# Delta-rule attention feeding a squared-ReLU MLP on one core: when the MLP's weights are split, by which engine, and in whose scratch

## The chip, the cores and the metric

One NeuronCore of a Trainium2 chip runs the whole program. The metric is device time in microseconds (us). The engines are TensorE (PE in the profile, its weight loads PEld), VectorE (DVE), ScalarE (ACT), GpSimd (POOL) and the queue of SyncE (SP), which issues nearly all DMAs.

## The reference

There are 4 batches of 8 heads, 768 time steps and head dimension 48, all float32.

```python
k_n = k / (norm(k) + 1e-6)
for t in range(768):                       # for each batch and head; state is 48 x 48
    y[t] = q[t] @ state
    v_old = state.T @ k_n[t]
    state += beta[t] * outer(k_n[t], v[t] - v_old)
x = y as (3072 tokens, 384)                # 8 heads x 48
out = square(max(x @ w_in, 0)) @ w_out     # w_in 384 x 2048, w_out 2048 x 384
```

## The kernel before, in words

**Attention.** Time is cut into 12 units of 64 steps, and two units make a pair. For a pair, `key_products` (L377) multiplies the keys with themselves on PE and copies four sets of blocks out of PSUM (`copies`, by ACT, DVE or both, after the string `A["copies"]`). `prepare` (L417) turns one result on DVE and makes norms and betas. `invert` (L468) inverts 32-row triangles by substitution, two DVE instructions a step. `ended` (L496) scales and turns the inverse. For the first pair alone (FAST), `invert` works on 16-row halves in 15 steps (31 for the other pairs), and `corrected` (L520) joins the halves: PE, a copy on ACT, PE twice more, then two DVE subtractions into `tt` and `t1` (L542, L543). `below` (L547; `below_both` for later pairs) makes the blocks under the diagonal. `query_products` (L600), `scale_v` (L625) and `state_part` (L635) then give a unit's `w`, the new state and `y`, strictly in order of units.

**MLP.** `moe(u)` (L688) takes the 256 tokens of unit u. Every float32 operand is the sum of a high and a low fp32r part, and each product is three matmuls. For each of 8 blocks `fp` it forms h (L735), evacuates it by three ACT passes (L742, L743, L745) and one DVE pass (L710, `rest`), and two blocks later multiplies by w_out (L719, `second`).

**Weights.** The weights come in 17 parts (`weight_parts`), 14 of 768 columns and 3 of 512, in the order in which moe(0) wants them. `fetch` issues their DMAs on SP. `split_weights` is a generator that turns a raw part into its high and low half:

```python
ACT  a    = |raw| * 2**-112              # L222   (magnitude)
ACT  tail = low bits of raw, scaled      # L224   (magnitude)
DVE  a = (a << 3) | tail                 # L252   join 1
DVE  a = (raw & sign) | a                # L257   join 2
ACT  high = a as fp32r                   # L260
low = a - high: DVE, L238 (mode "d"), or PE twice and an ACT copy, L234 and L236 (mode "t", parts 0 to 3)
```

`a` lies in a ring of three buffers and `tail` in one of two, so a part's two ACT passes run at most two parts ahead of its joins. `half_of` makes moe wait, at build time, until a part's steps have been issued.

**Order.** PE, SP, DVE and ACT run in the order in which the program is written (`manual_schedule`). The first unit is issued by the string `A["order"]`, a letter per piece (A and B key products, P prepare, I a step of the inverse, e ended, c corrected, b below, V scale_v, s state_part); after piece n, `A["fill"][n]` steps of the split are issued, 40 of its 51 before moe(0) begins. From unit 1 on, `weave` sorts pieces of attention and of the MLP of the unit before by the fractions in `A`: moe(0) is woven with attention of unit 1, moe(1) with unit 2, and so on. The rest of the splits and the first pair's `corrected` and `below` of unit 1 lie in the first weave, and the second pair's inverse (31 steps) in the first and second; in the second weave, `below_both` waits for `ended` of that pair.

## Time and profile before

| | |
|---|---|
| median of 3 runs | 607.59 us (607.03, 607.59, 609.38) |
| profiled execution | 606.13 us, of which the span from first to last instruction is 604.4 us |
| PE busy, mean granted clock | 557.8 us (92%), 0.964 of full speed |
| DVE busy, ACT busy, POOL busy | 393.3 us (65%), 331.0 us (55%), 49.2 us (8%) |
| DMA | 37.77 MB, mean 62 GB/s |

A row of the timeline gives start and duration in us, engine, line, operation and operands; square brackets hold the engine's idle time just before the row and what ended it. Line numbers are those of the kernel before. A row of the windows gives, for a stretch, its length and for each engine the busy time and the number of instructions in brackets, then the granted TensorE clock, the DMA share and GB/s.

### The profile page before, as it was taken

What the parts mean: (1) busy time and instruction counts of PE and PEld (TensorE: products, weight loads), DVE (VectorE), ACT (ScalarE), POOL (GpSimd) and SP (SyncE); (2) the same over time, 40 slices, a digit from 0 to 9 for tenths busy, and PEclk for the clock granted to TensorE, in tenths of its full rate; (3) what the DMA queues carried; (4) which work ended last, traced back from release to release, by engine and by line L of the source; (5) the groups of instructions that cost most, each with busy time, mean ns of one, the idle gap of its engine ahead of it and who ended that gap; (6) DMA issues with size and microseconds to landing.
All of it is one profiled execution on the core that took longest, in us unless ns stands there. A gap on an engine that the chain in (4) does not pass through costs nothing.

```text
span 604.4 us, 23205 instructions
## 1 busy us (share of the span) xinstructions
PE 557.8 (92%) x10520; PEld 535.2 (89%) x10520; DVE 393.3 (65%) x709; ACT 331.0 (55%) x521; POOL 49.2 (8%) x62
## 2 busy tenths in 40 slices
PE   4554589999999999999999999999999999999997
PEld 3434479999999999999999999999999999999997
DVE  2996986989446989257988348996548895421111
ACT  4774987444646454557354556355456365454442
POOL 3110000200101102002002002002002002001000
PEclk9695599999999999999999999999999999999999
DMA  8996160032243050253050251140450320200101
GB/s 245 301 264 218 23 114 3 2 69 41 29 74 62 2 102 6 29 88 49 9 99 2 43 92 30 35 73 3 65 81 19 61 48 4 49 8 2 27 1 26
DMA packets 146674, 37.77 MB, mean 62 GB/s; under 512 B 140272, under 2 KB 143344, under 8 KB 146576
## 3 DMA queue, kind: packets, MB, share of 16 engines
q1 hardware_dynamic: 146496, 36.20, 29.4%
q8 instruction: 82, 1.34, 0.9%
q14 instruction: 16, 0.13, 0.1%
q10 hardware_dynamic: 80, 0.10, 0.0%
HBM read 31.56 MB, written 4.72 MB: 60 GB/s over the span
## 4 chain that ended last, share of the span: by engine, by line
PE 88%; ACT 3%; DVE 3%; DMA 2%; SPq 2%; issue 2%; DVEq 0%; ACTq 0%
PE h L735 35%; PE o L719 32%; PE g L719 2%; PE g L655 2%; PE g L645 2%; PE g L607 2%; PE g L680 2%; PE g L661 2%; PE g L387 2%; PE g L673 2%; SPq L304 1%; PE h L695 1%; DMA tt<-in_k_dram 1%; DMA ap<-in_k_dram 1%; PE g L538 1%
## 5 line engine op out<-in xcount | busy, mean ns | idle before, releaser
L719 PE MATMUL o<-w,h_h 128*128 128x384 f32 x704 | 185.5, 344 | 0.0
L735 PE MATMUL h<-x_h,w 128*128 128x256 f32 x1152 | 170.5, 283 | 2.3 <-DVE x_l L698 1.7
L735 PEld LDWEIGHTS h<-x_h,w 128*128 128x128 f32 x1152 | 154.4, 190 | 4.0 <-ACT x_h L697 2.6
L710 DVE TENSOR_TENSOR h_l<-r,h_h 128x512 fp32r<-128x512 f32 x96 | 68.3, 715 | 116.4 <-ACT h_h L745 116.4
L742 ACT ACTIVATE r<-h 128x512 f32<-128x512 f32 x96 | 57.4, 598 | 124.4 <-PE h L735 111.6
L719 PEld LDWEIGHTS o<-w,h_h 128*128 128x128 f32 x704 | 121.2, 189 | 2.2
L719 PE MATMUL o<-w,h_l 128*128 128x384 f32 x352 | 118.2, 336 | 0.0
L735 PE MATMUL h<-x_l,w 128*128 128x256 f32 x576 | 100.4, 283 | 0.6 <-issue 0.6
L735 PEld LDWEIGHTS h<-x_l,w 128*128 128x128 f32 x576 | 82.6, 191 | 0.8 <-issue 0.8
L719 PEld LDWEIGHTS o<-w,h_l 128*128 128x128 f32 x352 | 66.1, 188 | 0.0
L743 ACT ACTIVATE r<-r 128x512 f32<-128x512 f32 x96 | 60.7, 633 | 3.1
L745 ACT CAST h_h<-r 128x512 fp32r<-128x512 f32 x96 | 59.6, 621 | 3.0
L491 DVE TENSOR_TENSOR z<-z,tmp 128x31 f32<-128x31 f32 (+15 forms) x155 | 53.2, 343 | 5.3
L489 DVE TENSOR_TENSOR tmp<-lt,z 128x31 f32<-128x31 f32 (+15 forms) x155 | 52.6, 340 | 3.8
L613 POOL TENSOR_SCALAR_AFFINE_SELECT ap<-ap 64x1024 f32<-64x1024 f32 x24 | 30.6, 1277 | 242.7 <-ACT ap L610 241.9
L676 DVE TENSOR_TENSOR state<-state,g 48x768 f32<-48x768 f32 x22 | 20.9, 950 | 21.0 <-PE g L673 20.9
L683 ACT COPY y<-g 128x768 f32<-128x768 f32 x12 | 9.6, 800 | 38.7 <-PE g L680 38.7
L434 POOL MEMSET z<- 128x1024 f32 x5 | 4.8, 953 | 233.9 <-DVE lt L422 191.9
L697 ACT CAST x_h<-h 128x384 fp32r<-128x384 f32 x24 | 11.4, 481 | 19.2 <-PE h L695 19.2
L698 DVE TENSOR_TENSOR x_l<-h,x_h 128x384 fp32r<-128x384 f32 x24 | 13.0, 556 | 13.3 <-ACT x_h L697 12.9
L260 ACT CAST w<-a 128x768 fp32r<-128x768 f32 (+1 forms) x17 | 13.4, 796 | 9.7 <-DVE a L257 9.7
L661 PE MATMUL g<-vt,tt 64*64 64x48 f32 x768 | 14.8, 225 | 3.1 <-ACT tt L566 3.1
(152 smaller groups left out, 707.8 us busy)
## 6 DMA issues: line engine op xcount, KB each, us to landing
w<-in_moe_w_out_dram SPq DMA_DIRECT2D x8, 768.0 KB, 9.5
w<-in_moe_w_in_dram SPq DMA_DIRECT2D x6, 768.0 KB, 7.2
vt<-in_v_dram SPq DMA_DIRECT2D x48, 96.0 KB, 3.0
kp<-in_k_dram SPq DMA_DIRECT2D x48, 96.0 KB, 3.1
out_dram<-rest SPq DMA_DIRECT2D x47, 96.0 KB, 2.2
kb<-in_q_dram SPq DMA_DIRECT2D x40, 64.0 KB, 2.4
kb<-in_k_dram SPq DMA_DIRECT2D x32, 64.0 KB, 2.7
w<-in_moe_w_in_dram SPq DMA_DIRECT2D x3, 512.0 KB, 5.1
```

The source lines that it names most:

```text
L260: nc.scalar.copy(out=hl[:, 0], in_=a.bitcast(F32))
L489: nc.vector.tensor_tensor(out=tmp, op=ALU.mult, in0=lt[:, s:s + 1, s + 1:].broadcast_to([P, nj, nt]), in1=z[:, :nj, s:s + 1].broadcast_to( ...
L491: nc.vector.tensor_tensor(out=z[:, :nj, s + 1:], in0=z[:, :nj, s + 1:], in1=tmp, op=ALU.subtract)
L613: nc.gpsimd.affine_select(out=half, in_=half, pattern=[[0, 2 * X], [1, C]], base=0, channel_multiplier=-1, compare_op=ALU.is_gt, fill=0.0)
L661: nc.tensor.matmul(ps[half_rows(b ^ j), j, x], lhsT=t[half_rows(b), j, x], rhs=vt[half_rows(b), j, x], start=True, stop=True)
L676: nc.vector.tensor_tensor(out=s[dims(j)], in0=s[dims(j)], in1=ps[dims(j)], op=ALU.add)
L710: nc.vector.tensor_tensor(out=h_l, in0=r, in1=h_h.bitcast(F32), op=ALU.subtract)
L719: nc.tensor.matmul(o[i], lhsT=a[:, e, i * P:(i + 1) * P], rhs=w_[w], start=(ft == 0 and n == 0), stop=(ft == FT - 1 and n == 2))
L735: nc.tensor.matmul(hp[:, e], lhsT=half_of(("wi", kt, part))[w][:, f], rhs=x[:, kt], start=(n == 0), stop=(n == 3 * KT - 1))
L742: nc.scalar.activation(out=r, in_=hp, func=AF.Relu)
L743: nc.scalar.activation(out=r, in_=r, func=AF.Square)
L745: nc.scalar.copy(out=h_h, in_=r)
```

## The change

The split's two ACT passes (`magnitude`) leave the generator of the joins. They get their own counts, `A["fillm"]`, and may run far ahead: parts 0 to 4 put `a` and `tail` not into the rings but into the rooms of parts 8, 9, 10, 11 and 15, which are fetched only after the owner's halves are made. The raw parts 8 to 16 are therefore issued one or a few at a time as parts 0 to 4 end, no longer 17 in one go ahead of `corrected`.

Engines are chosen per part by three letters: the magnitude (A is ACT, D is DVE), the cast to the high half (A or D), the low half (D is DVE, P is PE). Of 17 parts, three magnitudes (parts 1, 4, 8) and six casts (3, 5, 6, 8, 11, 13; the last of 512 columns) go from ACT to DVE, as `tensor_scalar` from SBUF to SBUF. The low halves on PE go from four parts to three (0, 1, 10). In the key products of the first pair one set of copies goes from DVE to ACT, in those of the second pair the set shared by both goes to ACT. One scaling of `goff` and one pair of upper copies in `below` go from ACT to DVE; the zeroing of `tt` goes from ACT to GpSimd.

In `corrected` the t1 product and subtraction are left out for the lower 32 rows of each 64: half of the L539 matmuls go, and one DVE subtraction on 128 partitions becomes two on 32. The first inverse and its scaled copy lie in a room of their own (`small`, zeroed and set by GpSimd at the start; it is the room of part 16). In unit 0 the state update follows y. The order string, all fractions and the fills are new: 26 of the 51 steps come before moe(0), the other 25 in the first 0.04 to 0.27 of the first weave. The string of `order` has 15 steps of the inverse as before.

```diff
-          'copies': {0: 'ADDA', 1: 'DADB', 2: 'ABDA'},
+          'copies': {0: 'DAAA', 1: 'DADA', 2: 'ABDA'},
-          'fill': [0, 0, 2, 2, 0, 1, 1, 1, 0, 0, 0, 0, 0, 0, 0, 0, 0, 0, 0, 0, 0, 0, 1, 1, 0, 1, 0, 0, 0, 0, 0, 0, 0, 2,
-                   0, 0, 1, 0, 0, 0, 1, 1, 1, 3, 3, 3, 0, 2, 2, 8, 3],
+          'fill': [0, 0, 0, 0, 1, 0, 0, 0, 0, 0, 1, 1, 0, 0, 1, 0, 0, 0, 0, 0, 0, 0, 0, 0, 0, 0, 0, 1, 0, 0, 0, 1, 1, 0,
+                   1, 0, 0, 0, 0, 0, 0, 0, 1, 4, 3, 1, 3, 0, 2, 3, 1],
+          'fillm': [0, 0, 1, 0, 0, 1, 0, 1, 0, 0, 0, 0, 0, 1, 0, 0, 0, 1, 0, 0, 0, 0, 1, 0, 1, 0, 0, 0, 0, 1, 1, 2, 0, 0,
+                    0, 2, 0, 0, 2, 0, 0, 1, 0, 0, 1, 1, 2, 0, 0, 2, 2],
-          'mode': 'ttttddddddddddddd',
+          'mode': ['AAP', 'DAP', 'AAD', 'ADD', 'DAD', 'ADD', 'ADD', 'AAD', 'DDD', 'AAD', 'AAP', 'ADD', 'AAD', 'ADD',
+                   'AAD', 'AAD', 'AAD'],
-          'order': '-01lABBTPAAPPBPP2xPPIIIGIIyZIIIPIIIIIIIeeeecccVbbss',
+          'order': '01-AlBPBPBTxAAPPGP2PPPIIIIIZIIIIIIIIyIIeeeecccbVbss',
...
+    room_of = {x: r for x, r in zip(range(NW), wide_rooms) if r >= x + A["rooms"]}
+    owner = {r: x for x, r in room_of.items()}
...
-            if x < NW:
+            if x < NW and (x not in owner or weight_parts[owner[x]][0] in halves) and (x < NW - 1 or ("ended", 0) in done):
...
+        if x in room_of:
+            both = wpool.tile([P, 2, n], I32, name=f"w{room_of[x]}")
+            a, tail = both[:, 0], both[:, 1]
+        else:
             a = spool.tile([P, PC], I32, name="a", bufs=3)[:, :n]
             tail = spool.tile([P, PC], I32, name="rest", bufs=2)[:, :n]
+        if A["mode"][x][0] == "D":
+            nc.vector.tensor_scalar(out=a.bitcast(F32), in0=raw[:, :, 1].bitcast(F32), scalar1=2.0 ** -112,
+                                    scalar2=None, op0=ALU.mult)
+        else:
             nc.scalar.activation(out=a.bitcast(F32), in_=raw[:, :, 1].bitcast(F32), func=AF.Abs, scale=2.0 ** -112)
...
-            nc.scalar.copy(out=hl[:, 0], in_=a.bitcast(F32))
-            if x + 2 < NW:
-                fetch(max(0, min(x + A["ahead"], NW) - len(raws)))
-                ready[x + 2] = magnitude(x + 2)
+            if A["mode"][x][1] == "D":
+                nc.vector.tensor_scalar(out=hl[:, 0], in0=a.bitcast(F32), scalar1=1.0, scalar2=None, op0=ALU.mult)
+            else:
+                nc.scalar.copy(out=hl[:, 0], in_=a.bitcast(F32))
...
-                    nc.tensor.matmul(ps[r, j, 1, x], lhsT=z[r, j, x], rhs=yt[r, j, x], start=True, stop=True)
+                    if n % 2 == 0:
+                        nc.tensor.matmul(ps[r, j, 1, x], lhsT=z[r, j, x], rhs=yt[r, j, x], start=True, stop=True)
...
-        nc.vector.tensor_tensor(out=t1[:, :, i, :, :QB], in0=t1[:, :, i, :, :QB], in1=ps[:, :, 1, :, :QB], op=ALU.subtract)
+        for b in range(2):
+            nc.vector.tensor_tensor(out=t1[up(b), :, i, :, :QB], in0=t1[up(b), :, i, :, :QB], in1=ps[up(b), :, 1, :, :QB],
+                                    op=ALU.subtract)
...
+        if not first:
+            update()
...
         nc.scalar.copy(out=y.rearrange("p n (q j e) -> p j (n q) e", j=2, e=D), in_=gy)
+        if first:
+            update()
...
+            magnitudes(next(fillm, 0))
             take(splits, next(fill, 0))
```

## Rows read from the trace of the kernel before

**Rows 1.** The page's span and its 40 slices of 15.1 us each.

```profile
span 604.4 us, 23205 instructions
...
PE   4554589999999999999999999999999999999997
...
DVE  2996986989446989257988348996548895421111
...
PEclk9695599999999999999999999999999999999999
```

**Rows 2.** Windows, by stage of the opening and after it, all engines.

```profile
27.30:40.80 13.50, 7.76 (x94) 5.78 (x93) 12.49 (x35) 10.86 (x17) 3.40 (x3) 0.94 1.06 333
...
46.20:57.60 11.40, 6.17 (x384) 5.68 (x384) 6.09 (x7) 5.22 (x7) 0.00 (x0) 0.50 0.74 280
57.60:66.20 8.60, 2.46 (x128) 2.06 (x128) 8.53 (x11) 6.79 (x10) 0.00 (x0) 0.50 0.02 4
66.20:78.50 12.30, 7.88 (x326) 7.09 (x327) 10.88 (x15) 10.86 (x17) 0.00 (x0) 0.71 0.39 73
78.50:88.90 10.40, 9.29 (x306) 8.82 (x307) 10.23 (x15) 9.31 (x15) 0.00 (x0) 1.00 0.60 99
88.90:97.70 8.80, 8.80 (x253) 8.32 (x255) 2.01 (x4) 7.02 (x13) 0.00 (x0) 1.00 0.12 15
97.70:153.70 56.00, 56.00 (x903) 54.87 (x894) 52.31 (x104) 27.49 (x45) 6.75 (x6) 1.00 0.18 31
153.70:604.40 450.70, 444.39 (x7975) 431.06 (x7974) 270.29 (x492) 233.15 (x368) 32.51 (x26) 1.00 0.24 41
```

**Rows 3.** Groups by line, 0 to 95 us: busy us, mean ns | idle before.

```profile
L257 DVE SCALAR_TENSOR_TENSOR a<-w,a 128x768 int32<-128x768 int32 (+1 forms) x17 | 15.4, 909 | 0.4
L252 DVE SCALAR_TENSOR_TENSOR a<-a,rest 128x768 int32<-128x768 int32 (+1 forms) x17 | 15.4, 906 | 1.4 <-ACT rest L224 1.3
L222 ACT ACTIVATE a<-w 128x768 f32<-128x768 f32 (+1 forms) x17 | 14.8, 871 | 2.1 <-PE o L234 1.7 <-DVE w L238 0.2
...
L260 ACT CAST w<-a 128x768 fp32r<-128x768 f32 (+1 forms) x17 | 13.4, 796 | 9.7 <-DVE a L257 9.7
L238 DVE TENSOR_TENSOR w<-a,w 128x768 fp32r<-128x768 f32 (+1 forms) x13 | 11.5, 891 | 0.0
```

**Rows 4.** Timeline of DVE at the end of the first correction.

```profile
57.64 0.42 DVE L542 TENSOR_TENSOR tt<-tt,g 128x256 f32<-128x256 f32 x1 [5.28 <-PE g L539]
57.98 0.41 DVE L543 TENSOR_TENSOR t<-t,g 128x256 f32<-128x256 f32 x1
...
60.04 0.95 DVE L252 SCALAR_TENSOR_TENSOR a<-a,rest 128x768 int32<-128x768 int32 x1
60.91 0.96 DVE L628 TENSOR_TENSOR vt<-vt,nr 128x768 f32<-128x768 f32 x1
```

**Rows 5.** Chain of waits, 40 to 92 us: start, us, what.

```profile
50.24 2.98 issue
...
55.20 1.48 issue
```

**Rows 6.** Timeline of DVE from the second pair's key products.

```profile
97.72 0.69 DVE L402 COPY z<-g 128x512 f32<-128x512 f32 x1 [4.46 <-PE g L387]
98.45 1.39 DVE L404 COPY z<-g 32x512 f32<-32x512 f32 x2
...
102.01 1.40 DVE L399 COPY mt<-g 32x512 f32<-32x512 f32 x2
```

**Rows 7.** Timeline, the narrow DVE instruction with a constant.

```profile
25.42 0.18 DVE L443 TENSOR_SCALAR n<-s 128x32 f32<-128x32 f32 x1
```

**Rows 8.** Timeline where the second pair's inverse is handed to PE.

```profile
151.62 2.06 DVE L516 STREAM_TRANSPOSE t<-z 128x1024 f32<-128x1024 f32 x1
...
155.73 0.21 PE L577 MATMUL g<-tt,mt 32*32 32x32 f32 x1
```

**Rows 9.** Timeline, the first MLP matmul of the kernel.

```profile
78.52 0.95 PE L735 MATMUL h<-x_h,w 128*128 128x256 f32 x6 [1.70 <-DVE x_l L698]
```

## The prediction, made before the changed kernel ran

> **What bounds the kernel now.** I read the page's slices first [rows 1]: PE is full from slice 7 to the last, and all that is not full lies in the first six slices, some 91 us. There DVE's digits are the high ones, with a 4 at 45 to 60 us and a 3 at 91 to 106 us. So the end of the run is set by how early PE becomes full, and by what it must still wait for after that.

> Then the windows by stage [rows 2]. After 153.7 us PE is busy for 444.4 of 450.7 us, and part of the rest is the tail. At most a few us are to be had there; I count nothing for the new fractions of the later units. From 97.7 to 153.7 us PE is busy for 56.00 of 56.00 us, while DVE is busy for 52.31: DVE works at its limit on the second pair (preparation, 31 steps of the inverse, its turning), and hands over in time by little. The last turning ends at 151.62 + 2.06 = 153.7 us and PE's first matmul on it starts at 155.73 [rows 8]; PE had other work till then and lost nothing. If PE comes to that place earlier, it waits for DVE. So two clocks run in this opening: PE's, which starts with the first MLP matmul at 78.5 us [rows 9], and DVE's, which must end its work on the second pair. The later of the two decides.

> Of DVE's clock the windows show the holes. Between 27.3 and 153.7 us it is idle for 5.3 us in the first correction (6.09 busy of 11.40), for 6.8 us between the last weight and the second pair's key products (2.01 of 8.80), and in no other stage for more than about 1 to 4 us. Rows of the timeline give the same two: 5.28 us until PE's L539 ends [rows 4], 4.46 us until PE's L387 ends [rows 6].

> **The change, step by step, on DVE.** Into the holes goes weight work: 14 of the 51 steps, some 12 us at 0.87 each (below), that stood ahead of moe(0) now stand behind it. In the correction the fills put ten weight instructions on DVE (one after the turning, then 5, 4 and 1 steps' worth), some 8 us, where before DVE waited 5.3; and 25 steps instead of 11 lie in the first weave, so that DVE is still on weights when PE reaches the key products. I let 1 us of the 12.1 stay: 11.1 us won.

> What it adds to DVE until the second pair is turned:
> - Nine passes come from ACT. The trace has no wide DVE instruction with one SBUF input and a constant. From below they cost 0.18 us, the narrow one with a constant [rows 7]; from above 0.87 us, the distance of two wide ones that follow each other (60.04, 60.91) [rows 4]. The one row is near in kind and the other in width, so I take the middle, 0.52: 4.7 us (1.6 to 7.8).
> - One low half more on DVE (14 instead of 13): 0.87, as the distance above.
> - One goff scaling of 256 columns: 0.4, as L543 [rows 4]; from below 0.2.
> - The t1 subtraction, twice: one instruction of 0.41 becomes two on 32 partitions with as many columns. L404 takes 1.39 for two on 32 partitions, L402 0.69 for one on 128 of the same width [rows 6]: fewer partitions save nothing. 0.8.
> - Two upper copies of 512 columns: 0.69 each from PSUM as L404 [rows 6], by the narrow row 0.18 each: I take 0.9 for both (0.4 to 1.4).
> - Copies that leave: one set of the first pair, 0.69 + 1.39 = 2.1, and DVE's half of a set of the second, 1.4 (L399) [rows 6].

> Sum: 4.7 + 0.87 + 0.4 + 0.8 + 0.9 - 2.1 - 1.4 = 4.2 us more (0.4 to 7.8). DVE ends the second pair 11.1 - 4.2 = 6.9 us earlier (3.3 to 10.7). Against it stands that PE has more of its work behind that place: the fractions put it at (0.4682 - 0.0044) / 0.5731 = 81% of moe(1)'s pieces before and at (0.5355 - 0.0272) / 0.648 = 78% after; 2.5% of 31 pieces. From 78.5 us to the end twelve units take 525.9 us, 43.8 each, with 34 pieces and the attention in them, so a piece is at most 1.3 us and this at most 1.0, which I take. Net on this clock: 5.9 us (2.3 to 9.7).

> [...]

> **On PE's clock.** Ahead of the first correction (46.2 us) the letters and fills put 6 joins in place of 11, two moved passes, one copy set less and one scaling more: 5 x 0.87 + 2.1 - 1.0 - 0.4 = 5.0 us less DVE work; the first part of it waits for loads and ACT in any case, so I take 3.6. The correction lasts 11.4 us, of which PE stands 2.98 + 1.48 us at "issue" [rows 5] with nothing to wait for; 64 of its 384 instructions go, of 6.17 us busy [rows 2]: 1.0 us. From there to the state (8.60 us) DVE has 1.2 of corrections, 4.0 of weights and 0.9 for the values, 6.1: 2.5 us less. From the state to the first MLP matmul (12.30 us, DVE busy 10.88) DVE has 9.2: 1.7 us less. That is 8.8 us: the MLP starts at 69.7. From there the first three MLP blocks and the second correction need little of DVE, but each evacuation and h_l stands behind some weight steps. I take 0.5 us off: PE is 8.3 us ahead when it comes to the second pair. There it finds DVE only 5.9 ahead.

> **What costs nothing, and why.** The copies that ACT gains: it loses nine passes at about 0.8 to 0.9 [rows 3] and was busy for 5.22 of 11.40 in the correction [rows 2]; if that cover went, relu of moe(0) would come late by as much. The late fetches: a room is free when its owner's low half is made, parts 8 to 10 are issued from the inverse to the correction and the rest in it, and their ACT passes come at 60 us and later. The DMA engines stand at 0.02 in 57.6 to 66.2 us [rows 2], so there is room; if a part came late, ACT would wait with w and y queued behind that pass, and PE for them. On SP, values and keys of unit 0 now stand ahead of those parts instead of behind, which can only help. GpSimd's zeroing and setting run where it was idle. The state update moved behind y leaves 1.5 to 2 us of PE and DVE work to the time after y, where nobody waits before unit 1's state.

> **The sum.** The profiled execution: 606.13 - 5.9 = 600.2 (span 604.4 - 5.9 = 598.5 and 1.73 around it). The lowest of the runs shown lies 0.9 above the profiled execution (607.03), the median 1.5; I add 0.9: **601.1 us**.

> **Rivals.**
> 1. *PE's clock decides.* If the moved passes cost less than about 0.26 us, DVE adds under 9 x 0.26 - 0.5 = 1.8 us, and PE no longer waits at the second pair. For it: 0.18 for the narrow one [rows 7]. Against: 768 columns are 24 times as many. 606.13 - 8.3 + 0.9 = 598.7.
> 2. *DVE gets back what the holes give.* Passes at 0.87, and half of the correction's hole stays (2.6 us) since the joins there wait for ACT's passes or PE stands longer at "issue": 11.1 - 2.6 - (7.8 - 0.5) - 1.0 = 0.2, 606.8; with the passes alone 604.2, with the hole alone 603.7. For it: ACT stood 9.7 us waiting for L257 and DVE 1.3 us for L224 [rows 3], so the two engines do hold each other up. Against: ACT's passes now run ahead. No real gain, then: the work has only moved.
> [...]

> **Chances.** Forecast 0.45 (its own range 598.5 to 604.2), rival 1 0.19, rival 2 0.24, rival 3 0.12. The runs of this kernel differ by 0.4% and a median can tell some 0.5% (3 us) from no change. Faster by more: 0.44 + 0.19 + 0.04 of rival 2's lower end = 0.67; within: 0.01 + 0.20 = 0.21; slower: rival 3's 0.12. The range leaves out rival 3 and a little at the lower end: 596.5 to 607.2, which takes in both ends of DVE's added work, 606.8 of rival 2 and 2 us below rival 1.

> **What the new profile would show.** Right: DVE without a hole over 2 us from 13 us to the second pair's turning, that turning at about 147 us; the first MLP matmul at about 70; PE full until the place of `below_both` in the second weave and there a wait of some 2 us on DVE; moved passes near 0.5 us. Wrong: passes at 0.9 us or 0.2 us; "issue" waits over 5 us in the correction; ACT waiting for a late weight part; a granted clock of 0.50 after 85 us.

## The result, and the profile after

| | before | after |
|---|---|---|
| median | 608.68 us (606.52 to 610.15, 11 runs) | 601.58 us (599.99 to 605.94, 11 runs) |
| ratio after/before, 95% interval | | 0.9897, 0.9875 to 0.9918 |
| profiled execution, its span | 606.13, 604.4 us | 601.16, 599.4 us |

The kernel became 1.0% faster; 601.1 us was forecast. The page of the kernel after answers to [rows 1]; its slices are 15.0 us each.

```profile
span 599.4 us, 22921 instructions
...
PE   5655899999999999999999999999999999999997
...
DVE  2999599999347988348988448896548895421111
...
PEclk9675699999999999999999999999999999999999
```

DVE's two digits of 6 at 45 to 60 and 91 to 106 us (the prediction called them 4 and 3; the row has 6 in both) are 9 now, and one 5 has come at 60 to 75 us. PE is full from slice 6 on, not 7. The windows say by how much; they answer to [rows 2], with stages of the new kernel (columns as there).

```profile
40.00:60.00 20.00, 11.38 (x536) 10.07 (x536) 19.60 (x26) 9.01 (x13) 0.00 (x0) 0.53 0.77 277
...
68.00:76.00 8.00, 6.93 (x163) 6.44 (x165) 4.25 (x8) 3.02 (x5) 0.00 (x0) 0.57 0.72 134
...
85.00:96.00 11.00, 11.00 (x192) 10.71 (x190) 10.90 (x16) 10.84 (x18) 0.00 (x0) 1.00 0.21 25
96.00:112.00 16.00, 13.83 (x206) 12.86 (x205) 15.45 (x26) 10.84 (x19) 4.95 (x4) 1.00 0.01 2
149.50:599.40 449.90, 444.52 (x7981) 431.34 (x7980) 270.70 (x491) 233.30 (x368) 31.65 (x26) 1.00 0.24 41
...
13.10:149.46 136.36, 112.13 (x2299) 101.83 (x2292) 125.75 (x225) 85.82 (x134) 12.25 (x10) 0.84 0.46 120
```

The last row runs from DVE's first work to the end of the second pair's turning. The same stretch before ended at 153.68 and had DVE busy for 121.56 of 140.58 us: DVE has 4.2 us more work and 8.4 us less idle time. After 149.5 us hardly anything changed: PE is busy for 444.52 of 449.90 us, before 444.39 of 450.70 [rows 2], so this part is 0.8 us shorter. In 85 to 96 us PE, DVE and ACT are all full; in 96 to 112 us PE is idle for 2.2 us, where before it was never idle.

The timeline of DVE shows the moved pass, the two holes of more than 1 us that are left, and the turning; it answers to [rows 4, 8].

```profile
59.44 0.96 DVE L294 SCALAR_TENSOR_TENSOR a<-w,a 128x768 int32<-128x768 int32 x1
60.43 0.56 DVE L298 TENSOR_SCALAR w<-a 128x768 fp32r<-128x768 f32 x1
62.79 1.92 DVE L722 TENSOR_TENSOR state<-state,g 48x768 f32<-48x768 f32 x2 [1.80 <-PE g L719]
...
73.67 0.42 DVE L585 TENSOR_TENSOR tt<-tt,g 128x256 f32<-128x256 f32 x1 [3.65 <-PE g L580]
74.01 0.85 DVE L587 TENSOR_TENSOR t<-t,g 32x256 f32<-32x256 f32 x2
...
147.41 2.05 DVE L558 STREAM_TRANSPOSE t<-z 128x1024 f32<-128x1024 f32 x1
```

PE's timeline at the first MLP matmul, at the transposes of unit 1's y (my landmark for the experiments; 126.2 us before) and where the second pair's inverse reaches it, beside [rows 8, 9]:

```profile
69.44 0.58 PE L786 MATMUL h<-x_h,w 128*128 128x256 f32 x1
...
121.37 0.49 PE L746 MATMUL h<-eye,y 128*128 128x128 f32 x3
...
151.21 0.21 PE L622 MATMUL g<-tt,mt 32*32 32x32 f32 x1
```

PE is 9.1 us ahead at the first (78.52 before), 4.8 at the second, 4.5 at the third (155.73), and 5.0 at the end. So half of the early start is lost again before 121 us. The chain of waits shows where it runs:

```profile
47.44 7.75 DMA w<-in_moe_w_in_dram
...
67.55 1.52 issue
69.51 2.22 PE h L786 x9
73.60 2.15 PE h L786 x9
...
78.77 1.85 PE g L275 x6
80.61 1.08 PE h L786 x9
...
90.51 0.96 DVE a L294
```

From 59 to 83 us the end hangs mostly on PE: with "issue" (idle time for which the profile shows no releaser), with two groups of nine matmuls at a granted clock of 0.50 and 0.55 (2.22 and 2.15 us, against 1.08 for nine at 1.00), and with the low half of weight part 10 (L275). From 85 to 100 us it hangs on DVE alone. Ahead of that the chain passes through the late load of weight part 8 (first line): it landed at 55.19 us and DVE began on it at 55.25. DVE was busy for 19.60 of the 20.00 us around it, so nothing was lost, but this load has no room left.

### The profile page after: what moved, and what is told of

Read it like the earlier page. It is cut to its first block, busy times and chain, and to the rows that moved or that the text cites. A ratio compares the mean times of both kernels' runs of the same rounds, so it can differ in the third digit from the quotient of the medians.

```text
span 599.4 us, 22921 instructions
## 1 busy us (share of the span) xinstructions
PE 563.3 (94%) x10386; PEld 539.1 (90%) x10386; DVE 398.6 (66%) x719; ACT 324.1 (54%) x510; POOL 51.2 (9%) x63
## 3 DMA queue, kind: packets, MB, share of 16 engines
q8 instruction: 81, 1.33, 0.9%
## 4 chain that ended last, share of the span: by engine, by line
PE 81%; DVE 7%; DMA 2%; issue 2%; ACT 1%; SPq 0%
PE h L786 33%; PE o L770 29%; PE g L770 2%; PE g L700 2%; PE g L729 2%; PE g L690 2%; PE g L719 2%; PE g L706 2%; PE g L652 2%; PE g L431 1%; DMA w<-in_moe_w_in_dram 1%; PE h L746 1%; DVE w L279 1%; PE g L811 1%; DVE t L558 1%
## 5 line engine op out<-in xcount | busy, mean ns | idle before, releaser
L786 PE MATMUL h<-x_h,w 128*128 128x256 f32 x1152 | 172.5, 286 | 1.7 <-DVE x_l L749 1.1
L761 DVE TENSOR_TENSOR h_l<-r,h_h 128x512 fp32r<-128x512 f32 x96 | 65.5, 686 | 111.0 <-ACT h_h L796 110.9
L534 DVE TENSOR_TENSOR z<-z,tmp 128x31 f32<-128x31 f32 (+15 forms) x155 | 55.1, 355 | 5.3
L532 DVE TENSOR_TENSOR tmp<-lt,z 128x31 f32<-128x31 f32 (+15 forms) x155 | 54.5, 352 | 3.7
L749 DVE TENSOR_TENSOR x_l<-h,x_h 128x384 fp32r<-128x384 f32 x24 | 13.0, 556 | 12.1 <-ACT x_h L748 11.8
L729 PE MATMUL g<-w,ap 64*64 64x48 f32 x768 | 14.6, 226 | 1.7 <-ACT w L709 1.4
```

Source lines behind the costliest of these rows:

```text
L532: nc.vector.tensor_tensor(out=tmp, op=ALU.mult, in0=lt[:, s:s + 1, s + 1:].broadcast_to([P, nj, nt]), in1=z[:, :nj, s:s + 1].broadcast_to( ...
L534: nc.vector.tensor_tensor(out=z[:, :nj, s + 1:], in0=z[:, :nj, s + 1:], in1=tmp, op=ALU.subtract)
L729: nc.tensor.matmul(gy[half_rows(b), j, x], lhsT=ap[0][half_rows(b ^ j), j, x], rhs=w[half_rows(b ^ j), j, x], start=first and x == 0, stop ...
L761: nc.vector.tensor_tensor(out=h_l, in0=r, in1=h_h.bitcast(F32), op=ALU.subtract)
L786: nc.tensor.matmul(hp[:, e], lhsT=half_of(("wi", kt, part))[w][:, f], rhs=x[:, kt], start=(n == 0), stop=(n == 3 * KT - 1))
```

## The experiments

Each kernel is the changed one with one edit. The time to set a ratio against is 0.9897; 0.001 is 0.6 us.

**The nine passes back on ACT.**

```diff
-          'mode': ['AAP', 'DAP', 'AAD', 'ADD', 'DAD', 'ADD', 'ADD', 'AAD', 'DDD', 'AAD', 'AAP', 'ADD', ...
+          'mode': ['AAP', 'AAP'] + ['AAD'] * 8 + ['AAP'] + ['AAD'] * 6,
```

> The changed kernel with the nine moved passes (three magnitudes, six casts) back on ACT, all else as changed. Theory A, DVE's clock decides: they took 0.56 us each on DVE (0.49 from start to start), so DVE ends the second pair's turning about 4.5 us earlier (145 in place of 149.5 us) and the run is 2 to 3.5 us faster than the changed kernel (598 to 599.5). Theory B, ACT is as full as DVE: it was busy for 11.11 of 11.30 us in 85.0 to 96.3 us, and gets 9 passes of 0.83 to 0.91, some 7.7 us; joins, relu and casts then wait for ACT, and the time is that of the changed kernel or up to 4 us slower (601 to 605).

Measured: 604.14 us, ratio 0.9918 (0.9896 to 0.9941). The transposes of unit 1's y came at 123.2, 1.8 us later. The window of 85 to 96 us, all engines:

```profile
85.00:96.00 11.00, 10.61 (x184) 9.83 (x183) 9.92 (x14) 10.87 (x19) 0.00 (x0) 1.00 0.28 35
```

DVE has holes again (9.92 busy) and ACT is full (10.87). The nine passes were 4.9 us of DVE's busy time, and taking them off brings nothing: up to 150 us DVE then waits 2.6 us for ACT's passes and 2.0 us longer than in the changed kernel for the state update on PE, and the second pair's turning ends 1.9 us later (151.3). By the ratios the move was worth some 1.3 us. The two intervals overlap, so the times alone do not show it; the landmark agrees.

**Less and more work on DVE.**

```diff
+            if x < 9:                              # less: second join of parts 9 to 16 left out
+            for _ in range(1 + (x >= 9)):          # more: done twice
             nc.vector.scalar_tensor_tensor(out=a, in0=raw[:, :, 1], scalar=-0x80000000, in1=a, ...
```

Each of the two lines is the edit of a kernel of its own.

> The changed kernel without the second join of parts 9 to 16: eight DVE instructions, five of 0.87 and three of 0.6 us from start to start, 6.1 us, are left out, so the signs of those weights are missing in the result. Theory A, DVE's clock decides: DVE ends the second pair 5 to 6 us earlier, PE's waits for DVE of some 3.5 us between 66 and 150 us go, and the run is about 3 us faster than the changed kernel (598), PE deciding after that. Theory C, PE alone decides (it runs at the low clock until 76 us and loses its lead there): the run stays within 1 us of the changed kernel (600.5 to 602).

> The changed kernel with the second join of parts 9 to 16 done twice (the second time changes nothing in the result): 6.1 us more on DVE while moe(0) runs. Theory A, DVE's clock decides: the run is 5 to 6 us slower than the changed kernel (606.5 to 607.5), all of what the change gained, and the wait shows on PE at or before the second pair's below. Theory C, PE decides and DVE has room: under 2 us slower (601.5 to 603.5).

Measured: 601.62 us, ratio 0.9881 (0.9863 to 0.9898), with 6.1 us less, and 607.63 us, ratio 0.9979 (0.9961 to 0.9997), with 6.1 us more. More costs 5.0 us. Less gives 1.0 at most: its interval takes in the changed kernel's 0.9897. The windows, first of the kernel with less, then of that with more:

```profile
85.00:96.00 11.00, 11.00 (x192) 10.80 (x191) 8.15 (x11) 10.81 (x18) 0.00 (x0) 1.00 0.19 24
```

```profile
85.00:96.00 11.00, 8.16 (x165) 7.18 (x164) 10.79 (x16) 8.77 (x14) 0.00 (x0) 1.00 0.16 21
```

With less, PE (11.00) and ACT (10.81) are still full and DVE idles; with more, PE idles for 2.8 us. The second pair's turning ends 5.2 us later with more (154.6), but only 0.8 us earlier with less (148.7): DVE then waits 4.8 us for the second correction, 3.65 in the changed kernel, and 4.7 us for ACT. So work added to DVE sets the end nearly in full; of work taken off, 1 us at most comes back before PE and ACT hold DVE.

**PE kept busy to raise its clock.** 21 unread matmuls of 512 columns were put between the pieces of the first unit.

```diff
+        BUSY = {('e', 3): 4, ('c', 0): 2, ('c', 2): 4, ('b', 0): 2, ('b', 1): 5, ('s', 0): 4}
...
+            for _ in range(n):
+                nc.tensor.matmul(t, lhsT=plus, rhs=halves[("wi", 0, 0)][0][:, :bank], start=True, stop=True)
```

> The changed kernel with 21 additional matmuls of 512 columns that nobody reads, put on PE after pieces of the first unit behind which PE waits (the end of the inverse, the correction, below, the state), 0.2 to 0.45 us each. Theory D, the low clock costs the lead: the granted clock is 1.00 in most of 45 to 76 us, where it was 0.50 to 0.69, the first MLP blocks take 1.1 in place of 2.2 us, DVE's wait of 3.65 us for the second correction shrinks to about 1.5, and the run is 2 to 4 us faster than the changed kernel (597.5 to 599.5). Theory A without D, DVE's own work sets the pace: the clock rises but the time stays (600.5 to 602.5), or the additional matmuls delay the chain and it is up to 3 us slower.

Measured: 604.65 us, ratio 0.9927 (0.9903 to 0.9952). Windows:

```profile
40.00:60.00 20.00, 15.81 (x545) 11.39 (x545) 19.59 (x26) 9.70 (x15) 0.00 (x0) 0.81 0.84 302
60.00:76.00 16.00, 12.24 (x471) 11.00 (x468) 9.66 (x14) 7.67 (x11) 0.00 (x0) 0.75 0.55 102
76.00:85.00 9.00, 9.00 (x177) 8.00 (x176) 8.63 (x13) 7.93 (x14) 0.00 (x0) 0.87 0.04 6
```

The clock rose from 0.53 to 0.81 in 40 to 60 us. But in 68 to 76 us, where the two slow groups of the MLP stand, it was 0.50 (0.57 in the changed kernel), in 76 to 85 us 0.87, not 1.00, and unit 1's y came 0.7 us later. The interval overlaps that of the changed kernel. The experiment does not tell what a full clock would be worth, only that it isn't had this way.

**Less work on PE, alone and with less on DVE.**

```diff
-                for w, x in ((0, x_h), (1, x_h), (0, x_l)):
+                products = ((0, x_h), (1, x_h), (0, x_l))[:1 if u == 0 and 3 <= fp <= 7 else 3]
+                for w, x in products:
...
```

> It leaves out the second and third of the three products of h in blocks 3 to 7 of the first MLP unit: 60 matmuls, at 1.08 us for 18 about 3.6 us less of TensorE's work between 83 and 108 us, nothing else. Theory 1 (the two clocks end within 1 us of each other; less work on one alone gives 1 us at most): 600.3 to 601.6. Theory 2 (TensorE alone decides, DVE only follows): 597.5 to 598.5. Theory 3 (DVE alone decides): 601.6, no change.

> The 60 matmuls left out and also the second join of weight parts 9 to 16 (6.1 us less on DVE). Theory 1 (two clocks near each other): now both end earlier, 3 to 4 us with what each gives alone, 597.3 to 598.6. Theory 2 (TensorE alone decides): the same as without the 60 matmuls alone, 597.5 to 598.5. Theory 3 (something else decides, such as ACT's passes on h or the units' order): 600.5 to 601.5.

The price in these expectations is wrong: 1.08 us is the time of nine matmuls (chain above), so 60 of them are 7.2 us. Measured: 604.67 us, ratio 0.9950 (0.9935 to 0.9964), and 603.99 us, 0.9936 (0.9920 to 0.9952): slower with less work, outside all three theories. Up to unit 1's y the runs go as two clocks near each other should: 121.4 in the changed kernel, 120.4 with less on DVE, 120.1 with less on PE, 119.2 with both. It was after that, in code that is the same, that 3.4 and 5.2 us were lost before unit 2's y (of the 5.2, 2.4 before PE reached the second pair's below). PE's timeline of the first of the two:

```profile
154.91 0.21 PE L635 MATMUL g<-tt,m 32*32 32x32 f32 x1 [0.47 <-issue]
158.64 0.39 PE L787 MATMUL h<-x_h,w 128*128 128x256 f32 x1 [0.69 <-issue]
162.53 0.43 PE L706 MATMUL g<-vt,tt 64*64 64x48 f32 x11 [0.19 <-issue]
166.08 0.49 PE L729 MATMUL g<-w,ap 64*64 64x48 f32 x17 [0.29 <-issue]
```

The windows between these points, and the same cut made in the changed kernel at its own stands in the opening (45.76, 51.13, 64.96 and 69.07 us):

```profile
154.86:158.59 3.73, 3.04 (x128) 2.79 (x128) 0.00 (x0) 2.30 (x3) 0.00 (x0) 1.00 0.42 55
158.59:162.48 3.89, 3.69 (x127) 3.31 (x128) 0.69 (x1) 1.85 (x3) 0.00 (x0) 1.00 0.02 4
162.48:166.03 3.55, 3.26 (x128) 2.82 (x127) 0.79 (x1) 0.80 (x1) 0.00 (x0) 1.00 0.02 5
```

```profile
45.71:51.08 5.37, 3.12 (x128) 2.59 (x128) 5.21 (x9) 2.56 (x3) 0.00 (x0) 0.50 0.93 320
51.08:64.91 13.83, 9.61 (x382) 8.52 (x382) 11.81 (x16) 8.11 (x12) 0.00 (x0) 0.50 0.59 220
64.91:69.02 4.11, 2.28 (x128) 1.88 (x127) 3.60 (x5) 2.56 (x4) 0.00 (x0) 0.92 0.72 128
```

Between two stands at "issue" lie 128 matmuls, or a multiple of it (382 is three times, two records missing), each with its weight load: 256 instructions. So it is in the kernel before, with 128 between the two of [rows 5], and in the other runs (127, 255, 382, 510, 638); one stand of 2.3 us, in the kernel without the rooms at 58.32 us, and a few of 0.16 us lie elsewhere. The list of DMA queues of the changed kernel has two that are named for instructions:

```profile
q8 instruction: 81, 1.33, 0.9%
q14 instruction: 16, 0.13, 0.1%
```

**No scratch in later parts' rooms.**

```diff
-          'rooms': 8,
+          'rooms': 99,
```

> No scratch in the rooms of later parts: parts 0 to 4 use the rings of three and two buffers like the others, and no load waits for an owner; order, fills and engines as in the changed kernel. Theory A (the rooms carry the gain, since ACT's passes can run ahead): ACT's passes wait for the rings, DVE's idle time before 62 us grows by 3 us and more, 604 to 607. Theory B (the order and the fills carry it; the rooms add little): 601.6 to 602.6.

Measured: 603.70 us, ratio 0.9935 (0.9921 to 0.9950), 2.3 us slower than with the rooms. DVE is busy for 25.02 + 17.17 us in 13 to 60 us, with the rooms for 25.56 + 19.60: 3.0 us more idle, as the first theory has it. The waits of PE between 40 and 85 us:

```profile
PE g L571 <- DVE t L558: 5.1, 1, 5.1
PE g L598 <- issue: 2.7, 1, 2.7
PE g L582 <- issue: 2.5, 1, 2.5
```

The turning that starts the first correction is waited for 5.1 us (1.9 in the changed kernel), and PE stands 10.7 us at issue, in all, against 3.1. PE's instructions are the same in both, so their number alone does not price the stands.

**The second correction one piece later.**

```diff
-  'corrected1': [0.0378, 0.0297, 0.0635], 'below1': [0.0758, 0.0825]
+  'corrected1': [0.0378, 0.0297, 0.08],   'below1': [0.09, 0.0967]
```

> The last step of the second correction and the two steps of below of unit 1 stand one MLP piece later in the first weave (0.08, 0.09 and 0.0967 in place of 0.0635, 0.0758 and 0.0825), so that DVE has two more weight instructions ahead of the subtraction it waited 3.65 us for. Theory 1 (that wait is a loss of DVE's clock, and DVE has 1 us at most to give): the wait falls below 2 us, the turning of the second pair ends 1.5 to 2 us earlier, and the time falls by 0.5 to 1: 600.6 to 601.1. Theory 2 (TensorE decides): wait smaller, time 601.6 as before. Theory 3 (the wait follows TensorE's slow pieces wherever it stands): still over 3 us, 601.6 to 603.

Measured: 602.29 us, ratio 0.9903 (0.9887 to 0.9920): no difference. DVE's wait fell from 3.65 to 1.3 us, as the first theory has it, and the second pair's turning ended 1.1 us earlier (148.4), but the time did not follow. Unit 1's y came at 120.3, 1.1 us early, and unit 2's at 166.6, as in the changed kernel: what was won was gone a unit later.

**The same work off PE, but every instruction kept.**

```diff
+                    cols = 32 if n and u == 0 and 3 <= fp <= 7 else 2 * P
...
-                        nc.tensor.matmul(hp[:, e], lhsT=half_of(("wi", kt, part))[w][:, f], rhs=x[:, kt],
+                        nc.tensor.matmul(hp[:, e, :cols], lhsT=half_of(("wi", kt, part))[w][:, f], rhs=x[:, kt, :cols],
```

> The second and third products of h in blocks 3 to 7 of the first MLP unit work on 32 of their 256 columns: the work of 60 matmuls goes as in e5_less_on_pe, but every instruction stays. Theory P (e5 lost its time because 120 instructions of TensorE left the stream, some 7.6 KB at 1.46 MB for the 23,205 instructions, which moves the places where it stands at issue): TensorE comes to the transposes of unit 1's y 1 us before the changed kernel (121.4) and stays ahead; the stretch from there to unit 2's y is 45.2 to 46.2 us, not 48.6; time 600.3 to 601.6. Theory Q (it lost because TensorE came early and thin, by clock or by collisions with loads): the stretch is 47.5 or more, 603.5 to 605.

Measured: 601.79 us, ratio 0.9907 (0.9872 to 0.9942; five runs at 601.5 to 602.0, one at 608.3). Unit 1's y at 120.8, unit 2's 45.4 us later, in the changed kernel 45.2, without the instructions 48.6. The windows of the kernel without the 60 matmuls, then of this one:

```profile
149.50:167.00 17.50, 15.85 (x567) 14.20 (x567) 5.01 (x6) 9.40 (x13) 0.00 (x0) 1.00 0.22 30
```

```profile
149.50:167.00 17.50, 17.50 (x583) 16.33 (x582) 6.43 (x7) 10.07 (x14) 0.00 (x0) 1.00 0.26 36
```

From the second pair's below to unit 2's y the same 568 matmuls take 15.4 us in the changed kernel (151.2 to 166.6) and 15.6 here (150.6 to 166.2). Without the 60 matmuls they start at 150.6 too, and at the same granted clock of 1.00, but take 18.1 us, with 1.65 at issue. So most of the loss lies in that stretch, and PE's arriving there early is not its cause.

But this kernel did not take the work off PE. Here are the starts of two groups of nine matmuls, first with six of the nine narrowed, then in the changed kernel:

```profile
86.44 0.76 PE L787 MATMUL h<-x_h,w 128*128 128x256 f32 x6
87.38 0.85 PE L787 MATMUL h<-x_h,w 128*128 128x256 f32 x6
```

```profile
86.64 0.87 PE L786 MATMUL h<-x_h,w 128*128 128x256 f32 x6
87.71 0.88 PE L786 MATMUL h<-x_h,w 128*128 128x256 f32 x6
```

The first group takes 0.94 us instead of 1.07, so ten groups save some 1 us and not 7.2; PE is busy for 23.84 us in 83 to 108 us, in the changed kernel for 23.73, without the instructions for 21.22. Two things therefore differ between the kernels, the instructions and nearly all of the work. Which of them made PE stand at issue after 154 us is not shown, and what less work on PE alone is worth was not measured.

**More instructions with hardly any work.**

```diff
+            for _ in range(16 if u == 0 and 3 <= fp <= 6 else 0):
+                nc.tensor.matmul(hp[:HB, 0, :HB], lhsT=ident[:HB, :HB], rhs=ident[:HB, :HB], start=True, stop=True)
```

> 64 matmuls of 32x32 are added ahead of blocks 3 to 6 of the first MLP unit, sixteen each, written over at once: 1 to 1.5 us of TensorE's work in a stretch where it stands idle for 3 us, but 128 instructions, half of the 16.4 KB that a packet of the instruction queue carries. Theory P (place of the stalls in the stream): the dense groups after 150 us stand at issue as without the 60 matmuls, stretch from unit 1's y to unit 2's 47 to 49 us, time 602.8 to 605. Theory Q (the place in the stream has no effect): stretch 45.2 to 46.2, time 601.5 to 602.6.

Measured: 603.90 us, ratio 0.9919 (0.9902 to 0.9936). The median is what the theory of the place in the stream wants, but its interval overlaps that of the changed kernel, and the trace is against it: 44.9 us from unit 1's y to unit 2's. By its stands the blocks did move as without the 60 matmuls: there a block began at a matmul of L635, at 154.91 us, here at one of the same line, at 155.98. But PE stood for 0.34 us and then no more. It stood at issue earlier, at 73.41 and 77.14 us. So the place in the stream alone does not bring those stands back. The profiled execution (602.08) is the fastest of the six; what the slower ones did after 150 us is not on record.

**The t1 correction on all rows again.**

```diff
-                    if n % 2 == 0:
-                        nc.tensor.matmul(ps[r, j, 1, x], ...
+                    nc.tensor.matmul(ps[r, j, 1, x], ...
-        for b in range(2):
-            nc.vector.tensor_tensor(out=t1[up(b), :, i, :, :QB], ...
+        nc.vector.tensor_tensor(out=t1[:, :, i, :, :QB], ...
```

> The t1 correction on all rows again: 64 matmuls of 32x32 more in each of the two corrections, and one DVE subtraction on 128 partitions in place of two on 32. Theory C (TensorE decides): about 1.0 us more in the first correction and 1 in the second, 602.6 to 603.8, first MLP matmul at 70.4. Theory D (DVE decides or the correction is hidden): DVE 0.4 us less per correction, 601.0 to 601.8.

Measured: 605.00 us, ratio 0.9940 (0.9926 to 0.9954): 2.6 us slower, more than either theory said, and as much as any of the three parts that were undone. PE's waits between 40 and 85 us, and the windows between the first stands (their ends):

```profile
PE g L580 <- issue: 6.1, 3, 2.8
PE g L605 <- issue: 3.3, 2, 2.1
PE g L581 <- issue: 1.8, 1, 1.8
```

```profile
45.55:49.83 4.28, 1.44 (x128) 1.32 (x128) 3.44 (x5) 2.58 (x3) 0.00 (x0) 0.67 0.87 310
49.83:55.75 5.92, 2.76 (x128) 2.23 (x128) 5.03 (x8) 1.50 (x3) 0.00 (x0) 0.50 0.99 379
```

PE stands 11.4 us at issue, in all, against 3.1. It does 1.44 us of work in a block of 4.28 us. The first MLP matmul is 0.5 us later (69.95), the second pair's turning 2.7 us. By the count of 256 the added matmuls (64, with as many weight loads) also move the ends of all later blocks, by half a block for each correction, so this does not tell how much of the 2.6 us is the matmuls and how much the new places of the stands.

**Half the columns in the second stage of the corrections.**

```diff
-  nc.tensor.matmul(ps[r, j, 0, x], lhsT=yt[r, j, x], rhs=z[r, j, x], ...
+  nc.tensor.matmul(ps[r, j, 0, x, QB:], lhsT=yt[r, j, x], rhs=z[r, j, x, QB:], ...
-  nc.tensor.matmul(ps[r, j, 1, x], lhsT=z[r, j, x], rhs=yt[r, j, x], ...
+  nc.tensor.matmul(ps[r, j, 1, x, :QB], lhsT=z[r, j, x], rhs=yt[r, j, x, :QB], ...
```

> In the second stage of both corrections each matmul works on the 16 columns that are read afterwards instead of 32; the number of instructions, and what is computed from them, stay. With the whole t1 the time had risen by 0.4% for 128 matmuls, and TensorE's time at issue between 40 and 85 us from 3.1 to 11.4 us. Theory K (it is the matmuls' columns that cost): 192 matmuls of the second stage took 4.8 us in the first correction, of it 1.0 at issue; half of the rest is won, 1.5 to 1.9 us for each of the two corrections, DVE's wait for the second one falls from 3.65 to about 2, and the time by 1 to 2.5: 599.1 to 600.6. Theory J (it is the instructions, and how they come to TensorE): the stage takes 4.3 to 5 us as before, at issue 3 us and more, time 601.2 to 602.6.

Measured: 602.16 us, ratio 0.9906 (0.9889 to 0.9922): no gain. The windows of the stage, first with 32 columns, then with 16:

```profile
42.88:47.71 4.83, 3.86 (x192) 3.62 (x192) 4.76 (x7) 1.93 (x3) 0.00 (x0) 0.50 0.61 176
```

```profile
42.37:47.90 5.53, 3.69 (x192) 3.53 (x192) 5.46 (x7) 2.35 (x3) 0.00 (x0) 0.52 0.75 245
```

It starts half a us earlier and ends later. PE stood from 44.15 to 45.97 us, with 32 columns from 44.79 to 45.76: it came to the end of the block earlier and waited for the next one all the same. So with 16 columns in place of 32 this stage was no shorter (5.53 us against 4.83). None of these versions is faster than the changed kernel beyond the intervals.

## Why the prediction was right, by its steps

- **DVE's added work**: forecast 4.2 us, measured 125.75 - 121.56 = 4.2. Of its terms, a moved pass of 768 columns starts 0.5 us ahead of what follows it (0.52 taken) and lasts 0.52 to 0.56; the two t1 subtractions take 0.85, two upper copies 0.84 (0.9 taken), goff 0.32 (0.4).
- **The holes**: 11.1 us forecast, 8.4 measured. The step that failed is "I let 1 us stay": the holes of [rows 4, 6] are gone, but a new one of 3.65 us came at the second correction and one of 1.80 at the state update, which the prediction had moved behind y as a thing that costs nothing.
- **The second pair's turning**: 6.9 us earlier forecast, 4.2 measured, the difference being those holes. The 1.0 us for the later position did not show: the end is 5.0 us earlier against 5.9.
- **The first MLP matmul**: 69.7 us forecast, 69.44 measured, but by luck: none of the parts came as forecast. Ahead of the first correction 5.6 us were won (3.6 forecast; its first matmul came at 40.66 us, before at 46.26), in the correction 3.1 (1.0 forecast; PE's stands there fell from 4.46 to 0.97 us), and from its end to the first MLP matmul only 0.4 (4.2 forecast). In this last part lies now the second stage of the second correction, which before came behind the first MLP matmul, and in it a stand of 1.5 us at issue.
- **"0.5 us off" between there and the second pair**: the worst-sized term. PE fell from 9.1 to 4.5 us ahead, 4.2 of it before unit 1's y. Up to there PE's busy time rose from 46.60 us (of 47.69) to 49.43 (of 51.93): 2.2 us by two groups at the low clock (0.50 and 0.55; 2.2 us for 1.08 each) and 1.85 by the low half of part 10, which the prediction did not price, less the t1 matmuls left out. Its idle time rose from 1.1 to 2.5 us, 2.1 of it waits for DVE in 96 to 121 us. At `below_both` it then waited for nothing, where some 2 us were forecast: it had already been held back further ahead.
- **Which clock decides**: DVE's, as forecast, for work that is added: 6.1 us more on it cost 5.0. For work taken off it is not DVE's alone: 6.1 us less gave 1.0 us at most, since DVE then waited for PE's second correction and for ACT. Less work on PE at the same number of instructions was not reached (1 us, not 7). In all kernels but the two without the 60 matmuls the span ends 449.9 to 452.2 us after the second pair's turning (454.7 and 453.2 there), so that turning tells the time fairly well; which engine held it up, it does not tell.
- **The t1 product**: forecast 1.0 us on PE's clock for 64 matmuls in the first correction, and nothing on DVE's. Undone in both corrections it cost 2.6 us. PE's busy time was the wrong price: 64 matmuls are half a block by the count above, and one block took 4.3 us there for 1.44 us of work.
- **What costs nothing**: in 13 to 150 us no engine waited for a late weight load or for GpSimd, though the load of part 8 came with nothing to spare (55.19 and 55.25 us). Of the copies that ACT gained, PE waited for one, 3.5 us until 20.39; in the kernel before it stood 5.8 us until 25.77, for a load. The rooms, to which the prediction gave no term of their own (they stand in the 11.1), were worth 2.3 us.
- **Rivals**: the first (PE alone) fell. The second (DVE gives it back) was partly true: of the 12.1 us of holes 3.7 stayed, net of the new ones. The third (the 0.12: PE starts early, but at a low granted clock) was true to 76 us: the clock was 0.53 in 40 to 60 us, 0.67 in 60 to 68, 0.57 in 68 to 76, and 1.00 in 76 to 85 and after.

The forecast came within 0.5 us because errors cancelled: the holes were 2.7 us too large, but the position cost of 1.0 did not come and 0.8 more was won behind the turning, and the median lies 0.42 us above the profiled execution where 0.9 was allowed. Undone one at a time, three parts cost 1.3 us (engines, not clear of the spread), 2.3 (rooms) and 2.6 (t1), each known to about 1.3. That they add up to nearly the whole 6.3 us is no proof that nothing else counts: without the rooms and without the t1 cut the loss shows in the same place, PE at issue in the opening (10.7 and 11.4 us), so the two may not add. What the new order and fills give by themselves was not tried.

## What to carry to other kernels

Do not price a stage of many small matmuls by PE's busy time alone: here 128 of them, with their weight loads, took 4.28 us for 1.44 us of work (the t1 correction on all rows). Look whether the trace has stands at "issue", and how many instructions apart; here most were 128 matmuls apart, or a multiple of it. Where two engines hand work to each other and both are near full, a load taken off one pays only up to the other's slack (here 1 us at most); test both directions, more and less, to see it. Look also whether an experiment took off what it was meant to: with six of nine matmuls narrowed a group still took 0.94 us of 1.07. Stands can differ far behind an edit: without the 60 matmuls of 83 to 108 us PE stood at "issue" four times from 154 to 166 us, for 0.19 to 0.69 us, the changed kernel not once. So a difference of half a per cent is to be read from landmarks in the trace beside the time.

## What the runs showed of the hardware

Nearly all of PE's stands at "issue" lie a multiple of 128 matmuls (256 instructions, 16.4 KB by the queue's 1.33 MB in 81 packets) apart, and no two successive ones of these ended less than 3.45 us apart: 3.45 in the correction of the kernel before [rows 5], 3.55 to 3.89 at 154 to 166 us with the DMA engines at 0.02 in two of the three cuts, and in the opening 3.73 (PE kept busy, 61.42 to 65.15 us, DMA at 0.19) to 6.47 (no rooms, 47.19 to 53.66 us, DMA at 1.00) where one block lies between. In the cuts shown above, blocks almost wholly of 32x32 matmuls held 1.44 us (t1 on all rows, granted clock 0.67) to 3.12 us (the changed kernel, 0.50) of PE's work. Between 40 and 85 us PE stood at "issue" for 2.1 us (less on DVE) to 11.4 us (t1 on all rows); that it waited for instructions there is the estimate made above. Whether the weight loads make the blocks late in the opening was not tried, nor is it known why the kernel without the 60 matmuls met stands after 154 us that the one with narrow matmuls did not.

The granted clock of the same stretch, 68 to 76 us, was 0.57 in the changed kernel and 1.00 in the one with 64 small matmuls added, although they stand behind that stretch, from 85.4 us on. Unit 1's y was no earlier for it (122.5 against 121.4): PE also stood at issue at 73.41 and 77.14 us, for 0.4 and 1.1 us.
